# Attention with decay and a sticky mixture of experts on one core: heads 4 to 7 of the first batch turned by TensorE instead of DMA transposes

## The chip, the core and the metric

The kernel runs on one core of one Trainium2 chip. TensorE (PE) multiplies matrices, VectorE (DVE), ScalarE (ACT) and GpSimd (POOL) work on elements, and SyncE (SP) issues nearly all of the DMA transfers, from one queue. The metric is the time of one execution in device microseconds, the median of several runs.

## The reference, cut to what matters

```
scores = (q @ k^T) / sqrt(64) + cum[i] - cum[j]       # cum: running sum of log f; causal; 8 batches, 8 heads, 576 x 64
attn   = exp(scores - max) / sum;   x = attn @ v      # heads joined: 8 x 576 tokens of 512
logits = x @ w_gate;  expert of a token: argmax of its logits, or the expert of the token before it if its local gate says so
out    = p[e] * (relu(x @ w1[e]) @ w2[e])             # 8 experts, 512 -> 1024 -> 512
```

## The kernel before, in words

Every product is made from f16 halves (a high and a low part). For the scores TensorE needs q and k with the head dimension on the partitions, and they arrive with tokens on the partitions, so each head has to be turned twice: once with high and low part together (128 rows, into `Aq` and `Ak`), and once as the high part alone (64 rows) with the decay rows below it (rows 64 to 69, into `QB` and `KB`). One unit of attention (`cunit`, `aunit`, `bunit`, `d1unit`) multiplies `Ak,Aq`, then `KB,QB`, adds a mask (these are its scores, lines 935 and 942), takes the maximum on VectorE (`nm`, L946), the exponential on ScalarE (`P`, L966), is turned on TensorE (`pt`, L981), split into `ph` (ScalarE, L986) and `pl` (VectorE, L990), and multiplied with V (`xp`, L960). Batch 0 has 20 units of heads 0 to 7 in order, five for each pair of heads, then four `d1unit`s and one `d2unit` for the last 64 tokens. Two pools of PSUM banks feed them: `psS` (four banks: scores, and the 64-row turns of heads) and `psT` (two banks: `pt`, and the 128-row turns).

In batch 0, `heads` turns heads 0 and 1 before the first unit and `due_head` turns heads 2 and 3 between units: four 64-row turns (`turn_high`), a product that writes the decay rows (`add_decay`), four 128-row turns (`turn_first`), a copy by VectorE to `Aq` or `Ak` and one by ScalarE to `QB` or `KB` (`untwist`). Heads 4 to 7 go another way: GpSimd splits them (`pieces`), `turn` turns them by DMA transposes on SP's queue, `copy_hi` copies the high part from `Aq` and `Ak` to `QB` and `KB` by DMA, and `aug_main` fills in the decay rows from a copy in DRAM. In batch 1 and later, `prep_turned` turns groups of eight blocks on TensorE and a DMA copies the high part in two halves (heads 0 to 3, heads 4 to 7) and a last piece.

The order on each engine is made when the program is built. `issue` takes, time after time, the stage of a unit that could start first by a model of engine clocks; the list `DUE` names steps (`k2`: `due_head(2, "k")`; `v`, `v4`: a split of V by ScalarE and VectorE; `a`, `b`: the lists `ORDA` and `ORDB`) with a model time, at which a step is put ahead of whatever stage comes next. `ORD0`, `ORDA` and `ORDB` are written by hand: `q:p` splits the last tokens of q, `q0:m` loads half of batch 1's q, `q:t4` and `q:c` are the DMA transposes and copies of heads 4 to 7, `0:R` and `1:R` copy constant rows, `q0:P` is a half of batch 1's split, `q:2` loads for batch 2. Engines then run their lists strictly in that order.

Of the kernel before, what the change touches and what calls it, by code (L numbers as in the profile page):

```python
# [10 lines left out]
F16 = mybir.dt.float16  # L11
I32 = mybir.dt.int32
AF = mybir.ActivationFunctionType
ALU = mybir.AluOpType
# [25 lines left out]
def moves_of(d):  # L40
    return [tuple(x.split(":")) for x in d.split()]

ORD0 = moves_of("q:l :k2 :sv k:l q:t4 k:t4 :sp q:p q0:m k:p q:c k:c q1:m q:t q:M k:t :lm k:m :at 0:R 1:R :lv")
ORDA = moves_of("k:M q0:P 0:V 1:V k:ag")
ORDB = moves_of("q:ag q:G0 2:V q1:P k0:P k1:P k:e q:e 3:V q:G1 k:G0 :vl :Vl k:G1 q:2 :iv v0:P k:2")

GM, GW = 8, 500

# [23 lines left out]
SB = 3  # L74

T0 = 9700.0
DUE = (("k2", 11000), ("q2", 12500), ("k3", 14500), ("q3", 15000), ("v", 18000), ("v4", 19500), ("a", 26000), ("b", 30000))

TUNE = {
# [23 lines left out]
def kernel(  # L103
# [12 lines left out]
    nc = tc.nc  # L116
# [117 lines left out]
                load_main(0, nm, C, h0, h1)  # L234


    for c in range(2):
        nc.gpsimd.memset(QB[0][64:70, 16 * c + 8:16 * c + 16], -1.0)

    lg = cp.tile([64, S], F32, name="lg")  # L240
    cu = cp.tile([64, S], F32, name="cu")
    spm = cp.tile([64, 3, 512], F16, name="spm")
    spt = cp.tile([64, 3, 64], F16, name="spt")
    one = cp.tile([1, 1], F32, name="one")
    nc.vector.memset(one, 0.0)
    nc.vector.memset(KB[0][64:70, 16:32], 1.0)

    spk = cp.tile([97, 512], F16, name="spk")
    nc.gpsimd.memset(spk, 0.0)
    nc.gpsimd.memset(spk[96:97], 1.0)  # L250
    pick = cst.tile([97, 2, 4, 6], F16, name="pick")
    nc.gpsimd.memset(pick, 0.0)
    for t in (pick[:, 0, :, 3:6], pick[:, 1, :, 0:3]):
        nc.gpsimd.affine_select(out=t, in_=t, pattern=[[-1, 4], [-32, 3]], compare_op=ALU.not_equal, fill=1.0, base=0,
                                channel_multiplier=1)
    nc.gpsimd.memset(pick[96:97, 0, :, 0:3], -1.0)
    nc.gpsimd.memset(pick[96:97, 1, :, 3:6], 1.0)
# [14 lines left out]
    def decays():  # L272

        x = lg[:, 0:512]
        nc.vector.tensor_copy(spm[:, 1], x)
        nc.vector.tensor_tensor(x, x, spm[:, 1], ALU.subtract)
        nc.vector.tensor_copy(spk[64:68], x[0:4])
        nc.vector.tensor_copy(spm[:, 2], x)

    def last_parts():  # L280
# [102 lines left out]
    def aug_main(b, nm, h0, eng=nc.sync):  # L383
        B, src = Tq[b][nm + "B"], augm[:, b * H + h0:(b + 1) * H]
        if nm == "k":
            eng.dma_start(out=flat(B[64:67, 4 * h0:32]), in_=src.rearrange("j h x -> j (h x)"))
        for c in range(2 if nm == "q" else 0):
            eng.dma_start(out=flat(B[67:70, 16 * c + 2 * h0:16 * c + 16]).rearrange("p (g x) -> p g x", x=64),
                          in_=src.rearrange("j h (a c x) -> j c (h a) x", a=4, c=2)[:, c])
# [207 lines left out]
    def turn_high(h, nm):  # L597
        st, c0 = psS.tile([128, 512], F32, name="st"), 64 * (nm == "k")
        for a in range(4):
            nc.tensor.matmul(st[0:64, 128 * a:128 * a + 128], lhsT=Tq[0][nm + "t"][:, 4 * h + a, c0:c0 + 64], rhs=ident16,  # L600
                             start=(a == 0), stop=True, skip_group_check=True)
        return st
# [21 lines left out]
    def start():  # L624
        for nm in "qk":
            new_prep(0, nm)
        high("q", 0, 2, True)
        high("k", 0, 2)
        high("k", 2, 4)
        high("q", 2, 4)  # L630
        other_masks()
        for h in range(2):
            low("q", h, h + 1, nc.gpsimd, True)
            low("k", h, h + 1, nc.gpsimd)
        low("k", 2, 4, nc.gpsimd)
        load_v(0, groups=((0, 2),), last=False)
        by_chunks()
        decays()
        for j in range(2):
            nc.scalar.copy(spk[32 * j:32 * j + 4], spm[0:4, j])  # L640
        for C in range(2):
            load_main(0, "q", C, 4, 8)
        put_aug()
        heads(0)
        low("q", 2, 4, nc.vector)
        heads(1)
        split_v(0, 2, True)
        for C in range(2):
            load_main(0, "k", C, 4, 8)
        load_v(0, groups=((2, 8),), last=False)  # L650
        for nm in "kq":
            aug_main(0, nm, 4)

        for nm in "qk":
            for x in pieces(nm, 4, 8):
                x()
        for nm in "qk":
            LT[1, nm] = LT[0, nm]
            new_prep(1, nm)
        for x in ORD0:  # L660
            moves(x)

    def same_rows(i):

        t, a, n, g = ((QB, 64, 6, 8), (KB, 67, 3, 16))[i]
        y = 36 // n
        nc.sync.dma_start(out=flat(t[1][a:a + 3]).rearrange("p (n y) -> p n y", n=n),
                          in_=flat(t[0][a:a + 3, g:g + y]).unsqueeze(1).broadcast_to([3, n, 128 * y]))
# [105 lines left out]

    def due_head(h, nm):
        t = max([clock["PE"]] + [e + WAIT[src, "PE"] for r in ("psS", "psT") for e, src in [min(room[r])]])
        st = turn_high(h, nm)
        add_decay(st, h, nm)
        pt = turn_first(h, nm)
        untwist(nc.vector.tensor_copy, Tq[0][nm + "A"], pt, 128, h, nm)  # L780
        untwist(nc.scalar.copy, {"q": QB, "k": KB}[nm][0], st, 70, h, nm)
        clock["PE"] = t + 870
        for r, eng, c in ("psS", "ACT", 480), ("psT", "DVE", 330):
            room[r].remove(min(room[r]))
            clock[eng] = max(clock[eng], t + 1000) + c
            room[r].append((clock[eng], eng))
# [114 lines left out]
    def compute(b, T):  # L901
# [273 lines left out]
        if b < B - 1:  # L1175
            then(max(lb, lc, key=UO.index), lambda: finish_main(b, X["xn"]))
        else:
            F = []

            def some():  # L1180
                F.extend(finish_main(b, X["xn"]))
                F[0]()
                F[1]()

            then(lb, some)
            then(lc, lambda: F[2]())
        for i, u in enumerate(units if b > 1 else ()):
            u["needs"] = [(b, x, min(i // 10 * 2 + 1, 4) if i < 20 else 4) for x in "qk"]
        return [units[i] for i in UO]
# [24 lines left out]
    def start_of(st):  # L1214

        n, u, prev = line[st][0]
        eng, _, _, takes, _ = u[st]
        t = clock[eng]
        after = []
        if st == "tq":  # L1220
            after.append((u["ready"], "POOL"))
        elif st == "z0":
            if "w0" not in EX or "xt0" not in EX:
                return None
            after += [(EX["w0"], "POOL"), (EX["xt0"], "POOL")]
        elif prev is not None or st not in ("sc", "z0"):
            dep = (n, prev) if prev is not None else (n - 1, "ex")
            if dep not in ends:
                return None
            after.append(ends[dep])  # L1230
        if st == "sc":
            for key in u.get("needs", ()):
                if key not in turned:
                    return None
                after.append((turned[key] + 3500, "POOL"))
        for r, c in takes.items():
            if len(room[r]) < c:
                return None
            after += sorted(room[r])[:c]
        return max([t] + [e + WAIT.get((src, eng), 200) for e, src in after])  # L1240
# [56 lines left out]
    def issue(*until):  # L1297
        while any(line.values()):
            ready = [(start_of(st), line[st][0][0] + RANK[st], st) for st in STAGES if line[st]]
            if chain:  # L1300
                ready.append((side_next()[0], serial[0] + RANK["side"], "side"))
                W["side"] = side_weight(*side_next())
            t, _, st = min((x for x in ready if x[0] is not None), key=lambda x: (x[0] + W[x[2]], x[1]))
            if due and due[0][0] <= t and all(room[r] for r in due[0][2]):
                due.popleft()[1]()
                continue
            let_go(t)
            if st == "side":
                side_issue(*side_next())
                continue  # L1310
            n, u, prev = line[st].popleft()
            eng, cost, fn, takes, frees = u[st]
            for r, c in takes.items():
                for _ in range(c):
                    room[r].remove(min(room[r]))
            now[0] = t
            fn()
            clock[eng] = t + cost
            ends[n, st] = t + cost, eng
            if st == "eq":  # L1320
                turned[u["key"]] = t + cost
            for r, c in frees.items():
                room[r] += [ends[n, st]] * c
            if (n, st) == until:
                return

    turned = {}
    now = [0.0]

    def ends_at(eng, cost):  # L1330
# [482 lines left out]
    def open_small():  # L1813
# [5 lines left out]
    DO = {"k2": lambda: due_head(2, "k"), "q2": lambda: due_head(2, "q"), "k3": lambda: due_head(3, "k"),  # L1819
          "q3": lambda: due_head(3, "q"), "v": lambda: due_v(2, 4), "v4": lambda: due_v(4, 6), "v6": lambda: due_v(6, 8),  # L1820
          "a": due_a, "b": due_b, "nop": nop}
    due.extend((T, DO[f], ("psS", "psT") if f in ("k2", "k3", "q2", "q3") else ()) for f, T in DUE)

    NE = CAP + EARLY

# [798 lines left out]
```

## Time and profile before

| | |
|---|---|
| median of 3 runs | 803.95 us (803.55 to 807.25) |
| the profiled execution | 800.73 us, span 798.9 us |
| busy share of the span: PE, DVE, ACT, POOL | 94%, 63%, 55%, 51% |
| granted TensorE clock, mean over the span | 0.997 |

The span is the profiled stretch of the core; the execution's time has 1.8 us around it. The exponentials of attention end at about half of the span; the experts fill the rest. The change touches the first 80 us.

### The profile page before, as it was taken

The page shows a single profiled execution, that of the slowest core. Times are in us where ns is not written, and L with a number is a line of the kernel's source. Part 1 is how long each engine was busy: PE and PEld are TensorE (multiplying, and loading weights), DVE is VectorE, ACT ScalarE, POOL GpSimd, SP SyncE. Part 2 cuts the span into 40 slices and gives each one's busy share as a digit, 9 for nine tenths or more (in the row PEclk, how much of TensorE's full clock was granted, in tenths as well). Part 3 has the DMA queues.
Part 4 walks back from the last instruction along what each step waited for, and adds up shares of the span by engine and source line. Part 5 has one row for each costly group of instructions (what it writes and reads, how often), then busy time and mean ns, then how long its engine had stood idle before and what let it go on. Part 6 is the DMA issues. An engine that isn't in the chain of part 4 may idle for free. (4 is left out here: it accounts for less than half of the span.)

```text
span 798.9 us, 22025 instructions
## 1 busy us (share of the span) xinstructions
PE 752.1 (94%) x8972; PEld 542.0 (68%) x8972; DVE 503.0 (63%) x1142; ACT 435.6 (55%) x813; POOL 404.8 (51%) x471
## 2 busy tenths in 40 slices
PE   5799989999998989997899999999999999999996
PEld 3587878778787878875684565675665757666453
DVE  7688879799989899889969753352350524325010
ACT  5698968887786878776634224342341423324120
POOL 9698979295894869659617214121402213030101
PEclk9999999999999999999999999999999999999999
DMA  7967999686876868286495383775392744827101
GB/s 179 189 143 166 193 194 208 134 171 157 140 180 125 168 141 158 52 188 168 94 196 221 87 270 97 185 200 176 108 224 76 207 169 145 219 76 212 42 2 51
DMA packets 195338, 122.01 MB, mean 153 GB/s; under 512 B 135099, under 2 KB 171197, under 8 KB 195212
## 3 DMA queue, kind: packets, MB, share of 16 engines
q1 hardware_dynamic: 189169, 101.42, 56.0%
q0 software_dynamic: 6064, 19.14, 7.2%
q8 instruction: 72, 1.18, 0.6%
q14 instruction: 33, 0.27, 0.1%
HBM read 72.15 MB, written 19.36 MB: 115 GB/s over the span
## 5 line engine op out<-in xcount | busy, mean ns | idle before, releaser
L966 ACT ACTIVATE P<-st,nm 128x512 f32<-128x512 f32 (+3 forms) x288 | 152.8, 585 | 25.7 <-DVE nm L946 20.5
L1762 PE MATMUL z<-xT,wh 128*128 128x300 f16 (+7 forms) x832 | 144.6, 289 | 1.5 <-DVE hl L1749 1.5
L946 DVE TENSOR_REDUCE nm<-st 128x1 f32<-128x512 f32 (+4 forms) x264 | 134.1, 543 | 10.3 <-PE st L942 5.6
L986 ACT CAST ph<-pt 128x512 f16<-128x512 f32 (+1 forms) x200 | 115.7, 583 | 45.5 <-PE pt L981 41.2
L981 PE MATMUL pt<-ident,P 128*128 128x128 f32 x784 | 122.6, 279 | 8.2 <-DVE pl L990 5.4
L990 DVE TENSOR_TENSOR pl<-pt,ph 128x512 f16<-128x512 f32 (+1 forms) x171 | 114.3, 671 | 16.8 <-ACT ph L986 11.3
L1754 POOL DMA_INDIRECT out_dram<-o,ranki x23 | 23.9, 1039 | 160.3 <-ACT o L1753 139.0
L1749 DVE SCALAR_TENSOR_TENSOR hl<-z,hh 128x240 f16<-128x240 f32 (+7 forms) x64 | 42.2, 661 | 97.4 <-ACT hh L1748 97.4
L1789 PE MATMUL y<-uh,hh 128*128 128x512 f16 (+2 forms) x440 | 101.1, 311 | 0.0
L981 PEld LDWEIGHTS pt<-ident,P 128*128 128x128 f32 x784 | 84.3, 141 | 24.7 <-DVE pl L990 6.7
L1789 PE MATMUL y<-ul,hh 128*128 128x512 f16 (+2 forms) x440 | 100.8, 309 | 0.0
L1789 PE MATMUL y<-uh,hl 128*128 128x512 f16 (+2 forms) x440 | 100.8, 309 | 0.0
L1762 PEld LDWEIGHTS <-wh 128*128 128x128 f16 x832 | 81.0, 97 | 27.8 <-issue 2.1
L1762 PE MATMUL z<-xT,wl 128*128 128x300 f16 (+7 forms) x416 | 94.5, 289 | 0.0
L1789 PEld LDWEIGHTS <-hh 128*128 128x128 f16 (+2 forms) x880 | 56.8, 100 | 53.2 <-issue 5.2
L960 PE MATMUL xp<-VH,ph 128*128 128x65 f16 (+1 forms) x960 | 92.7, 196 | 0.0
L960 PE MATMUL xp<-VH,pl 128*128 128x65 f16 (+1 forms) x960 | 90.5, 194 | 1.8 <-DVE pl L990 1.7
L960 PE MATMUL xp<-VL,ph 128*128 128x65 f16 (+1 forms) x960 | 91.5, 195 | 0.0
L960 PEld LDWEIGHTS <-ph 128*128 128x128 f16 (+1 forms) x1920 | 83.3, 102 | 8.9 <-issue 4.9
L1748 ACT ACTIVATE hh<-z 128x240 f16<-128x240 f32 (+7 forms) x64 | 36.7, 574 | 93.5 <-PE z L1762 93.5
L935 PE MATMUL st<-KB,QB 70*128 70x256 f16 (+4 forms) x448 | 76.4, 278 | 5.1 <-DMA KB<-Ak 5.1
L935 PE MATMUL st<-Ak,Aq 128*128 128x256 f16 (+4 forms) x448 | 76.9, 281 | 2.4 <-ACT P L966 2.3
(369 smaller groups left out, 1404.9 us busy)
## 6 DMA issues: line engine op xcount, KB each, us to landing
stg<-in_moe_w_dram SPq DMA_DIRECT2D x64, 512.0 KB
xs<-xr SPq DMA_DIRECT2D x16, 512.0 KB
ldq<-in_q_dram SPq DMA_DIRECT2D x14, 512.0 KB
ldk<-in_k_dram SPq DMA_DIRECT2D x14, 512.0 KB
ldv<-in_v_dram SPq DMA_DIRECT2D x28, 256.0 KB
QB<-Aq SPq DMA_DIRECT2D x15, 256.0 KB
KB<-Ak SPq DMA_DIRECT2D x15, 256.0 KB
ldv<-in_v_dram SPq DMA_DIRECT2D x20, 64.0 KB
```

The lines of the kernel that those rows point to most:

```text
L935: nc.tensor.matmul(st[p0:p0 + m, co:co + n], lhsT=queries(lq, kk, h, c), rhs=rhs, start=(ps == 0 and first and co == col), stop=(ps == 1), ...
L946: nc.vector.tensor_reduce(dst, src, axis=AX.X, op=ALU.max, negate=True)
L960: nc.tensor.matmul(xo, lhsT=a[:, c0:c0 + m], rhs=w[:, vi, :], start=False, stop=(i == n - 1 and jj == 2), skip_group_check=True)
L966: nc.scalar.activation(P[:, c0:c1].rearrange("p (k x r) -> p k r x", r=2, x=64), st[:, c0:c1].rearrange("p (k r x) -> p k r x", r=2, x=64) ...
L981: nc.tensor.matmul(U["pt"][:, i * 128:(i + 1) * 128], lhsT=P[:, i * 128:(i + 1) * 128], rhs=ident, is_transpose=True, start=(i == 0), stop ...
L986: nc.scalar.copy(U["ph"][:, :cols], U["pt"][:, :cols])
L990: nc.vector.tensor_tensor(U["pl"][:, :cols], U["pt"][:, :cols], U["ph"][:, :cols], ALU.subtract)
L1748: nc.scalar.activation(hv, z[:, 0:nh, 0:wd], AF.Relu)
L1749: nc.vector.scalar_tensor_tensor(lv, z[:, 0:nh, 0:wd], 0.0, hv, ALU.max, ALU.subtract)
L1754: nc.gpsimd.indirect_dma_start(out=outf, out_offset=bass.IndirectOffsetOnAxis(ap=scat(t), axis=0), in_=o, in_offset=None, bounds_check=NT ...
L1762: nc.tensor.matmul(z[:, a, 0:wd], lhsT=w[:, d, fc * 128:(fc + 1) * 128], rhs=xT[:, x, a * wd:(a + 1) * wd], start=(i == 0), stop=(i == len ...
L1789: nc.tensor.matmul(y[m * r:m * r + m, 0:w], lhsT=a[:, fc, c0:c0 + m], rhs=u[:, fc, w * r:w * r + w], start=(i == 0), stop=(i == len(prods) ...
```

## The change

Heads 4 to 7 go through `due_head` too: eight more steps (`q4` to `q7`, `k4` to `k7`) stand in `DUE`, with model times around those of `k2` to `q3`, and the two splits of V come earlier in model time. The tile `pick`, which selects a head's decay rows, has eight heads in place of four. The DMA transposes, the DMA copies, the loads of decay rows and the constant rows (two memsets of 16 blocks in `QB` and `KB`) for heads 4 to 7 are gone. `same_rows` copies its constant rows from blocks of head 0 on, and the moves of batch 1 stand in another order. A unit of batch 0 is issued only when its heads have been.

```
-ORD0 = moves_of("q:l :k2 :sv k:l q:t4 k:t4 :sp q:p q0:m k:p q:c k:c q1:m q:t q:M k:t :lm k:m :at 0:R 1:R :lv")
-ORDA = moves_of("k:M q0:P 0:V 1:V k:ag")
-ORDB = moves_of("q:ag q:G0 2:V q1:P k0:P k1:P k:e q:e 3:V q:G1 k:G0 :vl :Vl k:G1 q:2 :iv v0:P k:2")
+ORD0 = moves_of(":k2 :sv q:l k:l :sp q:p q0:m k:p q1:m k:t q:t :lm q:M k:m :at :lv")
+ORDA = moves_of("k:M 0:V k:ag q0:P 1:V")
+ORDB = moves_of("0:R 1:R q:ag q:G0 q1:P 2:V k0:P k1:P k:e q:e 3:V q:G1 k:G0 :vl :Vl k:G1 q:2 :iv v0:P k:2")
...
-DUE = (("k2", 11000), ("q2", 12500), ("k3", 14500), ("q3", 15000), ("v", 18000), ("v4", 19500), ("a", 26000), ("b", 30000))
+DUE = (('k2', 11000), ('q2', 12500), ('k3', 14500), ('q3', 15000), ('q5', 15000), ('q4', 16000), ('k6', 16000), ('v', 16000), ('v4', 16500), ('k4', 17000), ('k5', 17000), ('q6', 20000), ('k7', 22000), ('q7', 23000), ('a', 26000), ('b', 30000))
...
-    for c in range(2):
-        nc.gpsimd.memset(QB[0][64:70, 16 * c + 8:16 * c + 16], -1.0)
...
-    nc.vector.memset(KB[0][64:70, 16:32], 1.0)
...
-        nc.vector.tensor_copy(spk[64:68], x[0:4])
+        nc.vector.tensor_copy(spk[64:72], x[0:8])
...
-        for nm in "kq":
-            aug_main(0, nm, 4)
...
-        t, a, n, g = ((QB, 64, 6, 8), (KB, 67, 3, 16))[i]
+        t, a, n, g = ((QB, 64, 6, 0), (KB, 67, 3, 0))[i]
...
+        headed.add((nm, h))
...
+            if any(x not in headed for x in u.get("heads", ())):
+                return None
...
+    for h in range(4, H):
+        for nm in "qk":
+            DO[f"{nm}{h}"] = lambda h=h, nm=nm: due_head(h, nm)
```

ScalarE's list shows how this comes out. Before, from the copy of q of head 2 on (`st` are turned heads and scores, `KB`, `QB` the targets of head copies, `P` the exponentials of units, `VH` the splits of V):

```order
L611 CAST QB_120<-st 70x4x2x64
L966 ACTIVATE P<-st,nm 128x4x2x64
L609 CAST KB_122<-st 70x512
L611 CAST QB_120<-st 70x4x2x64
L966 ACTIVATE P<-st,nm 128x2x64
L966 ACTIVATE P<-st,nm 128x3x2x64
L986 CAST ph<-pt 128x512
L318 CAST VH_124<-ldv 128x4x2x64
```

ScalarE's list of the changed kernel from the same place, the copy of q of head 2:

```order
L607 CAST QB_120<-st 70x4x2x64
L960 ACTIVATE P<-st,nm 128x4x2x64
L605 CAST KB_122<-st 70x512
L607 CAST QB_120<-st 70x4x2x64 x3
L605 CAST KB_122<-st 70x512
L314 CAST VH_124<-ldv 128x4x2x64 x2
L605 CAST KB_122<-st 70x512 x2
L607 CAST QB_120<-st 70x4x2x64
L605 CAST KB_122<-st 70x512
L607 CAST QB_120<-st 70x4x2x64
L960 ACTIVATE P<-st,nm 128x2x64
```

The eight new head copies and both splits of V stand together, right after head 3, ahead of the second unit's exponential. TensorE's list has the eight heads at the same place; before, after the last turn of head 3's q, it went on with the fourth unit's scores:

```order
L594 LDWEIGHTS t16q
L594 MATMUL pt<-ident_72,t16q 128x128
L935 LDWEIGHTS Aq
L935 MATMUL st<-Ak,Aq 128x256
L935 LDWEIGHTS Aq
```

In the changed kernel TensorE goes on, after the last turn of the last head (q of head 7), with those same scores:

```order
L590 LDWEIGHTS t16q
L590 MATMUL pt<-ident_72,t16q 128x128
L929 LDWEIGHTS Aq
L929 MATMUL st<-Ak,Aq 128x256
L929 LDWEIGHTS QB_120
```

So all eight heads are turned before the fourth unit's scores. Around the change of batches SP's list moves too. Before, it issued batch 1's copies of the high part of k (`KB_123<-Ak`: heads 0 to 3, heads 4 to 7, the last piece), then batch 2's loads (`ldq`, `ldk`, `ldv`):

```order
L422 DMA KB_123<-Ak 64x2048 x2
L429 DMA KB_123<-Ak 64x512
L192 DMA ldq<-in_q_dram 128x8x128 x2
L199 DMA ldq<-in_q_dram 64x4x64 x2
L192 DMA ldk<-in_k_dram 128x8x128 x2
L199 DMA ldk<-in_k_dram 64x4x64 x2
L212 DMA ldv<-in_v_dram 128x8x64 x4
```

SP's list of the changed kernel, with the same copies and loads:

```order
L418 DMA KB_123<-Ak 64x2048
L192 DMA ldq<-in_q_dram 128x8x128 x2
L199 DMA ldq<-in_q_dram 64x4x64 x2
L192 DMA ldk<-in_k_dram 128x8x128 x2
L199 DMA ldk<-in_k_dram 64x4x64 x2
L212 DMA ldv<-in_v_dram 128x8x64 x2
L418 DMA KB_123<-Ak 64x2048
L212 DMA ldv<-in_v_dram 128x8x64
L425 DMA KB_123<-Ak 64x512
```

The copy for heads 4 to 7 and the last piece now stand behind ten and eleven of batch 2's loads.

## Rows read from the trace of the kernel before

**Rows 1.** The page: the span, and busy time of the engines.

```profile
span 798.9 us, 22025 instructions
...
PE 752.1 (94%) x8972; PEld 542.0 (68%) x8972; DVE 503.0 (63%) x1142; ACT 435.6 (55%) x813; POOL 404.8 (51%) x471
```

**Rows 2.** Who waited for whom, 0 to 60 us: total, times, longest (us).

```profile
PE st L935 <- DMA KB<-Ak: 3.8, 1, 3.8
...
PE xp L960 <- DVE pl L990: 1.7, 1, 1.7
...
DVE ft L258 <- DMA ft<-in_f_dram: 0.7, 1, 0.7
```

**Rows 3.** Stretches: us; PE, PEld, DVE, ACT, POOL busy; PEclk, DMA share, GB/s.

```profile
35.00:40.00 5.00, 4.62 (x51) 4.23 (x50) 1.68 (x5) 2.13 (x5) 2.56 (x3) 0.66 1.33 222
...
65.00:70.00 5.00, 4.07 (x80) 3.06 (x77) 3.94 (x10) 4.13 (x9) 4.75 (x6) 1.00 0.34 72
70.00:75.00 5.00, 5.00 (x91) 4.11 (x88) 4.76 (x11) 4.05 (x10) 2.49 (x3) 1.00 1.14 280
...
80.00:100.00 20.00, 19.88 (x317) 16.40 (x315) 16.05 (x38) 18.26 (x37) 19.38 (x21) 1.00 0.93 194
100.00:120.00 20.00, 17.37 (x334) 14.72 (x333) 14.41 (x32) 13.67 (x30) 14.80 (x40) 1.00 0.95 194
```

**Rows 4.** Timeline of TensorE, 0 to 60 us: start, duration (us), instruction, count.

```profile
12.10 0.64 PE L600 MATMUL st<-ident,t16k 128*64 128x128 f16 x4
...
14.05 1.01 PE L605 MATMUL st<-spk,pick 97*6 97x512 f16 x2
15.00 0.51 PE L935 MATMUL st<-Ak,Aq 128*128 128x512 f16 x1
...
20.75 0.41 PE L600 MATMUL st<-ident,t16q 128*64 128x128 f16 x4
21.09 0.38 PE L605 MATMUL st<-spk,pick 97*6 97x512 f16 x1
...
21.63 0.38 PE L935 MATMUL st<-Ak,Aq 128*128 128x256 f16 x2
...
35.38 0.38 PE L935 MATMUL st<-KB,QB 70*128 70x512 f16 x1 [3.84 <-DMA KB<-Ak]
```

**Rows 5.** Timeline of ScalarE: a head copy, a V split, a turned group, `ph`.

```profile
21.50 0.58 ACT L611 CAST QB<-st 70x512 f16<-70x512 f32 x1 [0.61 <-PE st L605]
...
23.31 0.63 ACT L318 CAST VH<-ldv 128x512 f16<-128x512 f32 x1
...
64.56 1.03 ACT L514 ACTIVATE Ak<-st 128x1024 f16<-128x1024 f16 x1
...
68.57 0.59 ACT L986 CAST ph<-pt 128x512 f16<-128x512 f32 x1 [0.41 <-PE pt L981]
```

**Rows 6.** Timeline of VectorE: a head copy, two V splits, `pl`.

```profile
21.30 0.41 DVE L609 COPY Ak<-pt 128x512 f16<-128x512 f16 x1
...
23.97 1.57 DVE L319 TENSOR_TENSOR VL<-ldv,VH 128x512 f16<-128x512 f32 x1 [0.89 <-ACT VH L318]
...
26.66 0.68 DVE L319 TENSOR_TENSOR VL<-ldv,VH 128x512 f16<-128x512 f32 x1
...
66.50 0.68 DVE L990 TENSOR_TENSOR pl<-pt,ph 128x512 f16<-128x512 f32 x1
```

**Rows 7.** Timeline of SP's queue: issue start and duration (us), transfer, count.

```profile
29.55 0.51 SPq L422 DMA_DIRECT2D KB<-Ak  x1
...
68.05 1.23 SPq L192 DMA_DIRECT2D ldq<-in_q_dram  x2
...
76.80 4.84 SPq L212 DMA_DIRECT2D ldv<-in_v_dram  x4
```

**Rows 8.** Timeline of TensorE in batch 1: scores of its first unit and of head 4's first.

```profile
69.22 0.38 PE L935 MATMUL st<-Ak,Aq 128*128 128x512 f16 x1
...
78.11 0.39 PE L935 MATMUL st<-Ak,Aq 128*128 128x512 f16 x1
```

More of the change, by code (lines that the diff above doesn't have):

```diff
@@ L250 @@
     nc.gpsimd.memset(spk[96:97], 1.0)
-    pick = cst.tile([97, 2, 4, 6], F16, name="pick")
+    pick = cst.tile([97, 2, 8, 6], F16, name="pick")
     nc.gpsimd.memset(pick, 0.0)
     for t in (pick[:, 0, :, 3:6], pick[:, 1, :, 0:3]):
-        nc.gpsimd.affine_select(out=t, in_=t, pattern=[[-1, 4], [-32, 3]], compare_op=ALU.not_equal, fill=1.0, base=0,
+        nc.gpsimd.affine_select(out=t, in_=t, pattern=[[-1, 8], [-32, 3]], compare_op=ALU.not_equal, fill=1.0, base=0,
                                 channel_multiplier=1)
@@ L639, in start @@
         for j in range(2):
-            nc.scalar.copy(spk[32 * j:32 * j + 4], spm[0:4, j])
+            nc.scalar.copy(spk[32 * j:32 * j + 8], spm[0:8, j])
         for C in range(2):
@@ L1186, in compute @@
             then(lc, lambda: F[2]())
+        for i, u in enumerate(units[0:20] if b == 0 else ()):
+            h = i // 5 * 2 + (i % 5 > 1)
+            u["heads"] = [(x, y) for x in "qk" for y in ((h, h - 1) if i % 5 == 3 else (h,))]
         for i, u in enumerate(units if b > 1 else ()):
@@ L1302, in issue @@
                 W["side"] = side_weight(*side_next())
-            t, _, st = min((x for x in ready if x[0] is not None), key=lambda x: (x[0] + W[x[2]], x[1]))
+            able = [x for x in ready if x[0] is not None]
+            if not able:
+                due.popleft()[1]()
+                continue
+            t, _, st = min(able, key=lambda x: (x[0] + W[x[2]], x[1]))
             if due and due[0][0] <= t and all(room[r] for r in due[0][2]):
@@ L1327 @@
     turned = {}
+    headed = {(x, h) for x in "qk" for h in range(2)}
     now = [0.0]
@@ L1821 @@
           "a": due_a, "b": due_b, "nop": nop}
-    due.extend((T, DO[f], ("psS", "psT") if f in ("k2", "k3", "q2", "q3") else ()) for f, T in DUE)
+    for h in range(4, H):
+        for nm in "qk":
+            DO[f"{nm}{h}"] = lambda h=h, nm=nm: due_head(h, nm)
+    due.extend((T, DO[f], ("psS", "psT") if f[0] in "qk" else ()) for f, T in DUE)
     NE = CAP + EARLY
```

## The prediction

> **What bounds the kernel now.** I read the page first: TensorE is busy for 94% of the span, no other engine for more than 63% [rows 1]. So a saving counts where TensorE stands idle or runs slowly, and every microsecond of work added to TensorE is paid unless it falls into a gap. Then the list of waits for the first 60 us [rows 2]: two waits there touch the change. TensorE waits 3.8 us for the DMA copy `KB<-Ak`, the high part of k of heads 4 to 7; and it waits 1.7 us for a `pl`, whose engine, VectorE, has a split of V ahead of it (23.97, 1.57 us [rows 6]). Third, the table of stretches [rows 3]: from 35 to 40 us, behind that stall, the granted clock is 0.66 on the mean, while it is 1.00 around it: TensorE had stood idle, and part of this stretch ran at 1.2 GHz instead of 2.4. From 80 to 100 us TensorE is busy for 19.88 of 20 us and ScalarE for 18.26: in a steady batch nothing is left over in which lost time could be made up.
>
> **What goes.** The stall of 3.84 us ending at 35.38 [rows 4] goes, since `KB` of heads 4 to 7 no longer comes by DMA: -3.8. The slow clock behind it goes with it: 0.34 of 5 us of full-speed work were not done [rows 3], -1.7; if the clock fell for another reason it stays, so 0 to -1.7. The wait of 1.7 us for `pl` goes, because both splits of V now stand among the heads and no longer ahead of the first `pl`: -1.7, or 0 if the first units are held up by something else. The two memsets gone at the start give nothing: VectorE's first real operation waits for a DMA anyway (`ft`, 0.7 us [rows 2]), and everything up to TensorE's first head hangs on that; were this cover not there, VectorE's memset would count. The shorter DMA work of the first 30 us lets batch 1's loads start earlier; nobody in the rows waits for them.
>
> **What comes.** Eight heads' tensors on TensorE. One of them, q of head 3, takes from 20.75 to 21.63, 0.88 us, with nothing in the way [rows 4]; eight take 7.0 us. They stand in one block, ahead of the fourth unit's scores, where TensorE has no gap to hide them. ScalarE's copies are 0.58 us each and its two splits of V 0.63 [rows 5], together 5.9 us; VectorE's copies are 0.41 [rows 6], 3.3 us, and its two splits 1.4 to 3.1. Both fit beside 7.0 us, but the splits stand in the middle, behind the copy for k of head 6, and what is queued behind them are the copies of k of head 4. TensorE can go two tensors further, since two `psS` banks and two `psT` banks are free for heads (two `psS` banks hold scores). Counting forward with these durations, the third tensor behind the splits waits some 0.4 us for ScalarE, and then for VectorE 0.3 us where a split takes 0.68 and 1.9 us where it takes 1.57. The short one is the row at the time in question (26.66 [rows 6]), so I take 0.7 us in all: +7.7, bounds 7.0 and 9.3.
>
> Together the first batch gives 7.7 - 3.8 - 1.7 - 1.7 = +0.5 us. Bounds: 7.0 - 7.2 = -0.2, and 9.3 - 5.5 = +3.8 with the wait for `pl` not won back.
>
> On the clock in this block: heads 0 and 1 ran at the lower level (two `pick` products took 1.01 us at 14.05, where one took 0.38 at 21.09), and with just this mix of turns ahead of it the clock was at the higher level from the first scores on; head 3 was turned at it [rows 4]. The Trainium skill's page "TensorE: Matmul & The Clock Gate", Part 4 (PE-mode transpose), says on the other hand that the full clock does not engage for transposes; by it the run of heads would be turned at the slow rate, which is the third rival below. The trace does not bear it out for heads 0 to 3, whose nine matmuls hold four real transposes.
>
> **What moves.** SP's list around the change of batches is what I take most from. Batch 1's second copy of the high part of k (heads 4 to 7) stood ahead of batch 2's loads; now ten of them stand between it and the first copy. Call x the time at which SP issues the first of these loads, right behind the first copy, which it may issue once ScalarE has copied k's second group. From x SP needs, at the pace that it had for the same ten loads, 76.80 - 68.05 + 4.84/2 = 11.2 us [rows 7]. Then the second copy is issued. The one such copy that was waited for took from 29.55 [rows 7] to 35.38 [rows 4], 5.8 us, with loads in front of it in the queue. So it is usable at about x + 17.0. At the other end, by bytes alone: 4 x 512 + 4 x 64 + 2 x 256 KB of loads and 256 KB of the copy are 3.15 MB, which at 280 GB/s [rows 3] are 11.2 us.
>
> When does TensorE want it? Behind k's second group ScalarE has one more group (1.03), two `ph` (0.59 each [rows 5]) and VectorE one `pl` (0.68 [rows 6]) until the last full unit of batch 0 can be multiplied with V; with 0.6 us for those products batch 1's first scores come 3.5 us after the second group's copy, which is x + 2.9 (the first copy's issue takes 0.5 [rows 7]). Head 4's first scores came 78.11 - 69.22 = 8.9 us after batch 1's first [rows 8], so at x + 11.8. TensorE would then stand for 17.0 - 11.8 = 5.2 us by the one end and not at all by the other. SP's pace shows that the queue, not the bytes at their best rate, sets the time, so I go near the upper end, and somewhat below it because the copy of 29.55 had DMA transposes in the queue before it, which are gone: +4.0, bounds 0 and 5.2. What is queued behind that matmul is all of TensorE's list, so ScalarE and VectorE run dry as they did at 35 us. The stall is as long as the one that is removed, so I expect the same slow clock behind it: +1.7, bounds 0 and 1.7.
>
> The other moves I cost at nothing: the last tokens of q and k, the DMA transposes of those, the constant rows and the gate weights are issued earlier or at about their old time, and their users come some 20 us later; without that cover the price would be a DMA's issue to use, the 5.8 us above. GpSimd has two memsets less and starts batch 1's split earlier, for which nobody waited.
>
> **Sum.** +0.5 + 4.0 + 1.7 = +6.2 us. The profiled execution took 800.7 us (span 798.9), so 806.9 for one like it. The median of the runs shown is 803.95, 3.2 above the profiled one; the same difference laid on it gives 810.2, and I say 810. Differences below 0.5% (4.0 us) can hardly be told from none: the runs shown spread over 3.7 us.
>
> **Rivals.**
>
> 1. *The second copy of k lands in time*, since SP issues faster with fewer transfers in flight, or batch 1's start is later than I think against x. For it: the bound by bytes is x + 11.2, before the need at x + 11.8. Against it: SP's measured pace. Then the first batch's +0.5 is all: 804.5.
>
> 2. *Not slower: batch 1 flows better.* TensorE has gaps of 0.93 us between 65 and 70 us and of 2.63 us between 100 and 120 [rows 3], around the changes of batches. If GpSimd's and the loads' lead of some microseconds closes both, and the second copy is in time, the result is -0.2 - 0.9 - 2.6 = -3.7: 800.2. Point at which it decides: the copy is issued by x + 6.0 (11.8 - 5.8), so that nothing stalls. Against it: none of those gaps waits for GpSimd in the list of waits.
>
> 3. *The block of heads is slower than eight times 0.88.* By the clock at its lower level, two tensors took 15.00 - 12.10 = 2.90 us [rows 4], 1.45 each, 0.57 more than at the higher: 8 x 0.57 = 4.6, so 0.5 + 4.6 = +5.1 with no second stall: 809; with it above 814. The slow splits of V alone would bring +1.6 or, with the wait not won back, +3.3.
>
> **How the numbers follow.** The forecast, with a stall of at least 2 us in batch 1: 0.52. Rival 1: 0.27. Rival 2: 0.13. Rival 3: 0.08. The forecast's own range is 806.0 (a stall of 2 us, no slow clock behind it: +2.5 and half a microsecond of the first batch less) to 813.5 (+3.8 + 4.0 + 1.7); rivals 1 and 2 lie below. The range for 8 in 10 must reach rival 1 and part of rival 2 and leave out the worst sums: 802 to 813.5. Slower by over 0.5% is most of the forecast and rival 3: 0.47 + 0.08 = 0.55. Within 0.5%: the forecast's lower edge, rival 1 and some of rival 2: 0.05 + 0.25 + 0.03 = 0.33. Faster by over 0.5%: what is left of rival 2 and a little of rival 1 in which ScalarE rather than TensorE sets the pace: 0.12.
>
> **What the profile after would show.** The wait of TensorE for `KB<-Ak` at 31 us gone, and the granted clock at 1.00 from 15 us to the end of batch 0. A block of eight tensors of about 0.95 us each from 21.6 to 29.3 us, in it waits for ScalarE and VectorE of under 1 us. The fourth unit's scores at about 29.3, and batch 1's first scores near 70, 0 to 2 us later than before. Then the step that decides: some 9 us later a wait of TensorE for `KB<-Ak` of 2 to 5 us, SP issuing that copy some 11 us behind the first load of batch 2, and a clock below 1.00 behind it. I am wrong if that wait is not there (then rival 1 or 2), if the block of heads takes 12 us or its matmuls show the slow pace (rival 3), or if batch 1's first scores come before 68 us, for then TensorE had room that the busy rows do not show.

## The result, and the profile after

The changed kernel takes 809.98 us (median of 10 executions, 807.04 to 816.77) against 805.46 us (10 executions, 801.07 to 807.25): a ratio of 1.0068, 95% interval 1.0047 to 1.0089. It is slower: by 4.5 us between the medians, by 5.5 us by the ratio. Its profiled execution took 807.84 us with a span of 806.1, 7.2 above that of before. The lines of the kernel have moved: scores L935 is now L929, the turns L600/L594 are L596/L590, the copies of k on SyncE's queue L422/L429 are L418/L425.

The waits of TensorE in the changed kernel, first from 0 to 60 us, then from 66 to 150 us (total, times, longest):

```profile
PE st L596 <- ACT t16k L571: 8.2, 1, 8.2
PE st L601 <- ACT spk L636: 0.6, 1, 0.6
...
PE st L929 <- DMA KB<-Ak: 5.7, 1, 5.7
PE pt L975 <- DVE pl L984: 0.7, 2, 0.4
PE xp L944 <- DVE xn L1019: 0.3, 1, 0.3
```

Both waits of [rows 2] that the change was about, 3.8 us for `KB<-Ak` and 1.7 us for `pl`, are gone from the first list. The second is led by a wait for the same transfer one batch later, 5.75 us. It shows in TensorE's timeline (start, duration, instruction): the last turn of head 3 and the first of the eight new ones, the fourth unit's scores, and in batch 1 the first scores, head 4's first and the matmul that waited.

```profile
20.76 0.41 PE L596 MATMUL st<-ident,t16q 128*64 128x128 f16 x4
...
21.74 0.41 PE L596 MATMUL st<-ident,t16q 128*64 128x128 f16 x4
...
29.65 0.38 PE L929 MATMUL st<-Ak,Aq 128*128 128x256 f16 x2
...
68.39 0.38 PE L929 MATMUL st<-Ak,Aq 128*128 128x512 f16 x1
...
77.44 0.39 PE L929 MATMUL st<-Ak,Aq 128*128 128x512 f16 x1
...
83.58 0.58 PE L929 MATMUL st<-KB,QB 70*128 70x512 f16 x1 [5.75 <-DMA KB<-Ak]
```

Eight turns take 21.74 to 29.65, 7.91 us, 0.98 each with a single gap of 0.2. The fourth unit's scores came at 21.63 before [rows 4], so 8.02 us are spent; yet batch 1's first scores stand at 68.39 instead of 69.22 [rows 8]. The first batch gained 0.83 us. Everything is lost behind that, on SyncE's queue (issue start and duration, transfer, count):

```profile
65.63 0.48 SPq L418 DMA_DIRECT2D KB<-Ak  x1
66.16 1.52 SPq L192 DMA_DIRECT2D ldq<-in_q_dram  x2
67.74 3.05 SPq L199 DMA_DIRECT2D ldq<-in_q_dram  x2
70.83 2.15 SPq L192 DMA_DIRECT2D ldk<-in_k_dram  x2
73.02 2.30 SPq L199 DMA_DIRECT2D ldk<-in_k_dram  x2
75.43 1.95 SPq L212 DMA_DIRECT2D ldv<-in_v_dram  x2
77.47 1.84 SPq L418 DMA_DIRECT2D KB<-Ak  x1
```

The second copy of k's high part is issued at 77.47, behind ten loads of batch 2; TensorE had come to it at 77.83. The table of stretches (us; PE, PEld, DVE, ACT, POOL busy; PEclk, DMA share, GB/s) shows the rest:

```profile
35.00:40.00 5.00, 5.00 (x75) 4.37 (x76) 4.91 (x11) 4.70 (x12) 4.02 (x3) 1.00 0.98 244
80.00:85.00 5.00, 1.43 (x6) 0.86 (x5) 0.00 (x0) 0.00 (x0) 4.92 (x5) 0.59 1.01 182
85.00:90.00 5.00, 5.00 (x57) 4.33 (x57) 2.70 (x6) 3.04 (x6) 4.92 (x5) 0.73 0.76 140
100.00:120.00 20.00, 19.32 (x358) 16.33 (x358) 15.30 (x36) 17.79 (x37) 8.38 (x34) 1.00 0.68 140
```

From 35 to 40 us the clock is 1.00 (0.66 before [rows 3]); instead it falls while TensorE stands at 81 us, and TensorE works at 1.2 GHz until 87.7, some 4.2 us, of which 2.1 are lost. From 80 to 85 us VectorE and ScalarE do nothing: everything hangs on the one copy. From 100 to 120 us TensorE is busy for 19.32 us, 1.95 more than before.

**One instruction as a milestone.** ScalarE's turned group of k near 250 us is the same instruction in both kernels. These are its rows before and after, and in two runs told below (both copies first; old kernel with the late copy):

```profile
250.02 1.01 ACT L514 ACTIVATE Ak<-st 128x1024 f16<-128x1024 f16 x1
...
254.71 1.01 ACT L510 ACTIVATE Ak<-st 128x1024 f16<-128x1024 f16 x1
...
250.17 1.01 ACT L510 ACTIVATE Ak<-st 128x1024 f16<-128x1024 f16 x1
...
257.37 1.01 ACT L514 ACTIVATE Ak<-st 128x1024 f16<-128x1024 f16 x1
```

The changed kernel is 4.69 us late here: -0.83 + 5.75 + 2.1 = +7.0, and then -1.95 by two waits of the kernel before that it doesn't have:

```profile
109.22 0.42 PE L883 MATMUL st<-wg,xlt 128*64 128x18 f16 x8 [0.73 <-DMA xlt<-xl]
...
116.17 0.38 PE L935 MATMUL st<-KB,QB 70*128 70x512 f16 x1 [1.22 <-DMA KB<-Ak]
```

That makes 5.1; 0.4 I can't assign. Counted from batch 1's first scores, which takes out what differed earlier, the way to this row is 180.80 us before, 186.32 in the changed kernel, 182.77 and 187.43 in the two runs. By its end the profiled execution is 7.2 late; the 2.5 us beyond the milestone hold a stretch at the lower clock at 367 to 371 us, which before doesn't show, and two gaps of 0.43 us near 560 and 610 us that wait for nothing in the profile. No row ties them to the change.

### The profile page after: what moved, and what is told of

It reads as the page before. It is cut to its first block, busy times and chain, and to the rows that moved or that the text cites. A ratio compares the mean times of both kernels' runs of the same rounds, so it can differ in the third digit from the quotient of the medians.

```text
span 806.1 us, 22172 instructions
## 1 busy us (share of the span) xinstructions
PE 761.5 (94%) x9044; PEld 548.0 (68%) x9044; DVE 499.4 (62%) x1149; ACT 439.9 (55%) x821; POOL 403.8 (50%) x469
## 5 line engine op out<-in xcount | busy, mean ns | idle before, releaser
L929 PE MATMUL st<-KB,QB 70*128 70x256 f16 (+4 forms) x448 | 77.3, 280 | 5.7 <-DMA KB<-Ak 5.7
L929 PE MATMUL st<-Ak,Aq 128*128 128x256 f16 (+4 forms) x448 | 77.7, 283 | 2.0 <-ACT P L960 1.8
```

The costliest lines, as they stand in the source:

```text
L929: nc.tensor.matmul(st[p0:p0 + m, co:co + n], lhsT=queries(lq, kk, h, c), rhs=rhs, start=(ps == 0 and first and co == col), stop=(ps == 1), ...
```

## The experiments

The theory: the slower time is the late copy on SyncE's queue, not the turning of four heads on TensorE. The rival: the turns cost what the queue's wait seems to cost. Each run is compared with the kernel before on the same chip; the traces are of one execution each; "start" is batch 1's first scores (69.22 before, 68.39 after), "milestone" the row near 250 us.

**Both copies first.** The changed kernel, and where batch 1 begins:

```diff
         if b == 1:
+            let_go(1e12)
             while bulk and bulk[0][0] == 0:
                 bulk.popleft()[2]()
```

> The changed kernel (809.98 us) with one call added where batch 1 begins: both copies of k for heads 4 to 7 of batch 1 are issued on SyncE's queue ahead of batch 2's loads. Theory A (the late copy is what costs): the 5.75 us wait for KB<-Ak at the sixth unit of batch 1 is gone, and with it the half clock behind it (about 2 us): 7 to 8 us less than the changed kernel, 802 to 804.5 us, so level with the kernel before (805.46) or up to 0.5% faster. Theory B (the turning of heads 4 to 7 on TensorE costs what was gained, and the queue is only a shift): the wait closes but the time stays within 2 us of 810. Theory C (half of it): the loads of batch 2 are now later by the copies' issue (1 to 2 us) and the wait moves to batch 2: 805 to 808 us, with a new wait near the start of batch 2.

Measured: 806.68 us, ratio 1.0025 (0.9995 to 1.0056). The copies' wait is gone from TensorE's list, and so is the half clock at 81 us. Start 67.40, milestone 250.17: 4.54 us ahead of the changed kernel, level with the kernel before. But 0.99 of this was there before the added call acts: the fourth unit's scores stand at 28.66 in this execution and at 29.65 in that of the changed kernel. From start to milestone the call returns 3.55 us, half of theory A's 7 to 8. The time lies in theory C's range, and as in theory C a new wait stands near the change to batch 2, though for another transfer than its loads. TensorE's timeline of this run shows it:

```profile
108.86 0.51 PE L877 MATMUL st<-wg,xlt 128*64 128x18 f16 x8 [1.94 <-DMA xlt<-xl]
```

and behind it the clock falls (stretches of the same run, columns as above):

```profile
108.00:109.00 1.00, 0.14 (x4) 0.14 (x5) 0.00 (x0) 0.23 (x1) 1.00 (x2) 1.00 0.88 218
109.00:113.00 4.00, 4.00 (x52) 3.91 (x51) 0.30 (x3) 1.34 (x4) 0.60 (x1) 0.57 0.90 195
```

1.94 us of waiting and 0.43 of 4 us (1.7 us) of slow clock are new; the changed kernel had neither. Yet SyncE's queue issued the transpose `xlt<-xl` at about the same time before, in the changed kernel and in this run:

```profile
105.05 1.92 SPq L848 DMA_TRANSPOSE xlt<-xl  x1
104.64 1.30 SPq L842 DMA_TRANSPOSE xlt<-xl  x1
104.38 1.29 SPq L842 DMA_TRANSPOSE xlt<-xl  x1
```

In the changed kernel the queue had gone on while TensorE stood at 81 us, and so this transfer was in time there.

**The old kernel with the late copy.** The kernel before; on the queue the copy for heads 4 to 7 stands behind ten of batch 2's loads, as in the changed kernel (the last piece stays ahead of them):

```diff
-                    hold_back(ends_at(eng, cost), lambda: copy_hi(b, nm, 2 * j - 2, 2 * j + 2))
+                    hold_back(1e9 if (b, nm, j) == (1, "k", 3) else ends_at(eng, cost), lambda: copy_hi(b, nm, 2 * j - 2, 2 * j + 2))
...
+            if b == 1 and i == 2:
+                let_go(1e9)
```

> The kernel before (805.46 us) with only the queue's order of the changed kernel: the second copy of k for heads 4 to 7 of batch 1 is issued behind ten of batch 2's loads, heads 4 to 7 of batch 0 still by DMA. Theory A (that order alone makes the kernel slower): a wait for KB<-Ak of 5 to 6 us at the sixth unit of batch 1, and about 2 us of half clock behind it: 5.5 to 8 us more than before, 811 to 813.5 us. Theory B (the wait comes of the batch that runs earlier in the changed kernel, not of the queue): under 2 us more than before.

Measured: 811.83 us, ratio 1.0088 (1.0059 to 1.0118), theory A. TensorE's row in batch 1:

```profile
85.58 0.58 PE L935 MATMUL st<-KB,QB 70*128 70x512 f16 x1 [6.36 <-DMA KB<-Ak]
```

Start 69.94, milestone 257.37, 7.35 us late. Of this 0.72 stands at start already, ahead of the edit (the wait in the first batch was 4.60 us in this execution instead of 3.84); 6.63 come behind it. With heads 4 to 7 of batch 0 left to the DMA, the queue's order alone makes the kernel slower. And here too the two waits of before at 109 and 116 us are gone:

```profile
100.00:120.00 20.00, 20.00 (x338) 16.92 (x336) 15.10 (x34) 17.98 (x38) 8.37 (x34) 1.00 0.73 144
```

**The load behind.** The kernel before; half of batch 1's q (a load of 512 KB) stands behind the copies for heads 4 to 7 of batch 0:

```diff
-ORD0 = moves_of("... :sp q:p q0:m k:p q:c k:c q1:m q:t ...")
+ORD0 = moves_of("... :sp q:p k:p q:c k:c q0:m q1:m q:t ...")
```

> The kernel before (805.46 us) with one move changed: batch 1's q load of 512 KB, which stands ahead of the copies for heads 4 to 7 of batch 0 on SyncE's queue, stands behind them. Theory A (the 3.84 us wait for KB<-Ak in the first batch is the queue's): the wait shrinks by some 2 us (512 KB at about 245 GB/s), and the half clock behind it (1.7 us) shrinks or goes: 2 to 4 us less than before, 801.5 to 803.5 us. Theory B (the wait is for the transposes ahead of the copies): within 0.7 us of before.

Measured: 801.89 us, ratio 0.9974 (0.994 to 1.0008). The wait shrinks from 3.84 us [rows 4] to

```profile
32.60 0.38 PE L935 MATMUL st<-KB,QB 70*128 70x512 f16 x1 [1.58 <-DMA KB<-Ak]
```

and the clock stays at 1.00 from 35 to 40 us. The copy itself is issued no earlier than before (29.55 [rows 7]):

```profile
29.51 0.51 SPq L422 DMA_DIRECT2D KB<-Ak  x1
```

It is usable 3.1 us after its issue, against 5.8 before, with the load in front of it. Start 65.85, 3.37 us ahead; milestone 247.36, 2.66 ahead, with a new wait of 0.85 us at 55.29 for decay rows (`QB<-augt`) between. Theory A: 2.26 us of the wait and the slow clock behind it go with one move of one load, where the change spent 8 us of TensorE's time. The time agrees, but its interval reaches 1.

**Two heads.** As the run with both copies first, but heads 6 and 7 by DMA as before:

```diff
-ORD0 = moves_of(":k2 :sv q:l k:l :sp q:p q0:m k:p q1:m k:t q:t ...")
+ORD0 = moves_of(":k2 :sv q:l k:l q0:m q1:m q:t4 k:t4 :sp q:p k:p q:c k:c k:t q:t ...")
```

> As the run with both copies first, but only heads 4 and 5 of batch 0 are turned on TensorE; heads 6 and 7 go by DMA transposes and copies as in the kernel before, and land ahead of need by the queue's rows (needed about 44 us after the start). Theory A (TensorE sets the pace in the block of head units, 0.98 us a unit): four units less, 3.9 us less than the run with both copies first, 798 to 801 us. Theory B (ScalarE sets it, 0.48 us a unit): 1.9 us less. Theory C (the copies for heads 6 and 7 land late): a wait for KB<-Ak in the first batch of 2 to 4 us and its half clock, so level with or slower than the run with both copies first.

Measured: 803.88 us, ratio 0.9981 (0.9951 to 1.0012); against the run with both copies first 2.8 us less by the medians. Start 64.42 against 67.40: 2.98 us less. That lies between theory A's 3.9 and theory B's 1.9, and the time misses theory A's 798 to 801. Four turns at 0.98 are 3.92; of these 0.86 comes back as a wait right behind the block, where TensorE turns the first unit's exponentials,

```profile
25.65 0.65 PE L981 MATMUL pt<-ident,P 128*128 128x128 f32 x4 [0.86 <-DVE Ak L609]
```

which leaves 3.06. By the rows TensorE sets the pace inside the block (theory A's mechanism), and the copies for heads 6 and 7 are in time (no wait for `KB` in the first batch).

**V behind the heads.** As the run with both copies first, V's two splits due at 24.0 and 24.5 us instead of 16.0 and 16.5.

> As the run with both copies first, but the splits of V (due 16.0 and 16.5 us) are due after the last unit of heads (24.0 and 24.5 us), so that they stand behind the heads again. Theory A (their earlier place is what removed the wait for pl at the first pt of the first batch, counted 1.7 us): a wait of 1 to 1.7 us for pl or for VH is back between 22 and 32 us, and batch 1 starts 1.0 to 1.7 us later than in the run with both copies first. Theory B (the block of heads gives them time wherever they stand): no such wait, batch 1 starts within 0.4 us of it.

One execution, profiled: 810.29 us. Start 70.19, 2.8 us later than in the run with both copies first, more than theory A's 1.7. TensorE waits again, but for ScalarE's `P` and not for `pl`:

```profile
32.49 0.38 PE L929 MATMUL st<-Ak,Aq 128*128 128x512 f16 x1 [1.63 <-ACT P L960]
```

A piece of 0.5 us was there already when this run's heads began (17.60 for a turn that stands at 17.06 there), which leaves 2.3. The planner also put the fourth unit's scores ahead of the last two heads' turns here, so not all of it is V's. The 4.2 us that it waits for `xlt` in batch 1 add to its time. That the earlier place of V's splits pays is likely; how much is not shown by this one execution.

**V earlier in the old kernel.** The run with the load behind, V's splits due at 16.0 and 16.5 us.

> The kernel before with batch 1's q load behind the copies, and the splits of V due at 16.0 and 16.5 us; the transposes stay where they were. Theory A (a stall that goes shows again at the next late thing): the wait for pl of 1.18 us goes and the wait for KB<-Ak grows from 1.58 to 2.5 to 2.8 us, batch 1 starts within 0.4 us of the run with the load behind alone. Theory B: the wait for KB<-Ak stays below 2 us and batch 1 starts 0.8 us or more earlier.

One execution: 816.25 us. The wait for `pl` is gone and that for `KB` in the first batch is 2.66 us, as theory A has it, but start is 68.41, 2.56 us later. Behind 2.66 us the clock fell, where behind 1.58 it had not:

```profile
30.00:40.00 10.00, 7.34 (x73) 6.35 (x73) 4.12 (x9) 3.35 (x8) 4.56 (x7) 0.66 1.02 236
```

From the matmul that waited (32.74) the lower level lasts until 38.8 us, 6.0 us of work of which 3.0 are lost; that alone is more than the delay of start. Then SyncE's queue reads

```profile
67.23 0.48 SPq L422 DMA_DIRECT2D KB<-Ak  x1
67.77 1.53 SPq L192 DMA_DIRECT2D ldq<-in_q_dram  x2
...
76.59 3.67 SPq L212 DMA_DIRECT2D ldv<-in_v_dram  x3
80.36 1.02 SPq L422 DMA_DIRECT2D KB<-Ak  x1
```

and TensorE waits 5.74 us for that second copy. Neither theory had the slow clock or the second wait. No head was turned on TensorE here: two due times alone put the copy behind eleven loads. So the late copy isn't tied to the heads; the planner's clock in the program decides whether the copy is let go before the loads are sent, and in the kernel before it is.

**Transposes earlier, and with V.** The run with the load behind, and `q:t4 k:t4` ahead of `q:l k:l` (these two now behind `:k2 :sv`, as in the changed kernel); the second run has V's splits at 16.0 and 16.5 as well.

> The kernel before with batch 1's q load behind the copies, as in the run of that name, and with the DMA transposes for heads 4 to 7 of batch 0 issued ahead of the last chunks' loads of q and k instead of behind them. The q transposes can then be issued at 17.7 us (their input's end on GpSimd) instead of 19.96. Theory A: the 1.58 us that was left of the wait for KB<-Ak goes, batch 1 starts 1.3 to 1.6 us earlier than there, 800 to 801.5 us and so 0.5 to 0.7% under the kernel before. Theory B (GpSimd's pieces of the last chunk now wait for their late load, and the pieces and masks behind them): the wait goes but another of 1 us or more stands later in batch 0; 801 to 803 us.

> As the run with the transposes earlier, and the splits of V due at 16.0 and 16.5 us (before: 18.0 and 19.5). Theory A: the wait of 1.2 us for pl at 25.7 us goes too; with the copies 2.2 us earlier they still land about in time: batch 1 starts 0.8 to 1.2 us earlier than in that run, 799 to 800.5 us, 0.6 to 0.8% under the kernel before. Theory B (the stall only moves: TensorE reaches the copies 1.2 us sooner and waits for them as much longer): no change against that run.

Transposes earlier: 801.99 us, ratio 0.9962 (0.9941 to 0.9982), the only interval that lies below 1. But start is 65.91 and the wait for `KB` 1.81 us, much as with the load behind alone (65.85, 1.58): theory A's 1.3 us did not come. The copy of k is issued at 28.20 instead of 29.51, and is usable at 32.59 instead of 32.60. Whether this version is better than the load behind alone stays open. With V earlier: 811.98 us, ratio 1.0113 (1.008 to 1.0146); start 69.70, and a wait of 6.0 us for `KB` in batch 1, as in the run before. The late start has other reasons, also of that kind: waits of 2.2 us for `KB` (with the lower clock behind it, 0.83 from 30 to 40 us) and 2.5 us for `QB<-augt` in the first batch. Both theories fall.

**Held transfers first, everywhere.** Since the run with both copies first waited for `xlt<-xl`, which stands behind eight loads of batch 3, the rule was made general: whatever is held back goes ahead of every group of loads. Once on the run with both copies first, once on that with the load behind:

```diff
         while bulk and bulk[0][0] <= i and bulk[0][1]():
+            let_go(1e12)
             bulk.popleft()[2]()
```

> As the run with both copies first, and in every batch what is held back (copies of k, transposes of x) is issued ahead of the next group of loads, when a group is taken. Theory A (one queue is behind both waits: what the removed wait gave back in batch 1 was lost again because the transpose of xl stands behind eight of batch 3's loads): the wait for xlt of 1.94 us at 109 us and the half clock behind it go, and batch 2 begins 1.5 to 3.5 us earlier than in the run with both copies first; 803 to 805 us. Theory B (those loads are themselves needed in time: held to the side by the copies' waits they land later): the xlt wait goes and waits for ldq or KB of 2 us or more appear in batches 2 to 5; 806 to 810 us.

> The kernel before with batch 1's q load behind the copies, and with the same rule for what is held back as in the run just named. Theory A: its waits for xlt (1.16 us) and for KB in batch 2 (1.22 us) go, batch 3 begins 1.5 to 2.4 us earlier than in the run with the load behind alone; 799 to 801 us, 0.5 to 0.8% under the kernel before. Theory B as there: new waits of 2 us or more in batches 2 to 5; 802 us or more.

Measured: 832.08 us, ratio 1.0369 (1.0343 to 1.0395), and 823.15 us, 1.0259 (1.0228 to 1.0289): theory A falls in both, and B's 806 to 810 us is far too low for the first (the second meets B's 802 or more). The waits of SyncE's own queue in the first of the two, 75 to 125 us, show why:

```profile
SPq L422 <- DVE pl L985: 6.4, 1, 6.4
SPq L422 <- DVE Aq L513: 3.5, 1, 3.5
SPq L808 <- POOL t16q L354: 3.5, 1, 3.5
SPq L808 <- POOL t16q L358: 2.8, 1, 2.8
```

The queue stands still for transfers whose input isn't ready, and the loads stand behind them; the wait for `xlt` grew to 4.7 us. The planner's later choices changed too, so not all of the 25 us against the run with both copies first is laid to these waits.

**One move.** The clean form of that test: only batch 1's `xlt<-xl`, ready at 92.1 us, goes behind the first of batch 3's eight loads instead of behind all. The order on the other engines is the same row by row.

```diff
         while bulk and bulk[0][0] <= i and bulk[0][1]():
+            while ahead and any(x[2] is ahead[0][0] for x in held):
+                ahead.pop()[1]()
             bulk.popleft()[2]()
```

> As the run with both copies first, and a single move on SyncE's queue: batch 1's transpose xlt<-xl and the two stores of xl stand behind the first of batch 3's eight loads of q and k instead of behind all eight; no other engine's order differs by a row. Its input is ready at 92.1 us, so the queue does not stand still for it. Theory A (the queue's order is what the removed wait turned into): the 1.94 us wait for xlt at 109 us is gone, with it the half clock at 109 to 112 us (1.7 us): by 250 us it is 2 to 3.5 us ahead of the run with both copies first, 803 to 805 us. Theory B (batch 3's loads, now 2.8 us later, are the next to be late, or TensorE is held there by something else that is done at about the same time): under 1 us ahead by 250 us.

> The kernel before with batch 1's q load behind the copies, and the same single move of xlt<-xl. Theory A: its wait for xlt (1.16 us) is gone; the wait for KB in batch 2 (1.22 us) then grows by as much or stays, so 0 to 1.2 us ahead of the run with the load behind alone by 250 us: 800.5 to 802 us, 0.3 to 0.6% under the kernel before. Theory B: no change against that run, or later by 1 us or more.

On the run with both copies first: 804.04 us, ratio 1.0026 (1.0003 to 1.0048), the same as without the move. The wait for `xlt` is gone, and in its place stands

```profile
115.85 0.50 PE L940 MATMUL st<-KB,QB 70*128 70x512 f16 x1 [3.55 <-DMA KB<-Ak]
```

with the clock at its lower level behind it. Milestone 251.09, 0.92 us later than without the move: theory B. On the run with the load behind: 800.01 us, ratio 0.9977 (0.9953 to 1.0001); milestone 249.63 against 247.36, with two stretches of lower clock before it where that run had none. One of them, and 1.01 us of the delay, stand ahead of the edit: in this execution the first batch's wait for `KB` was 2.66 us instead of 1.58, and start 66.86. No gain is shown either way.

## Why the prediction was right, by its steps

The mechanism held: the removed waits are gone, and a stall for the late copy stands in batch 1. That 810 us was met to 0.02 is luck. The forecast was +6.2 us on a median of 803.95 (3 executions); measured are +4.5 on a median of 805.46 (10 executions). Three terms lie outside their own bounds, the first batch (-0.83, lower bound -0.2), the stall (5.75, upper bound 5.2) and the clock (2.1, upper bound 1.7), and a term of -1.95 was missing; these errors partly cancel.

- **What goes.** Right: wait of 3.84 us, slow clock of 1.7 and wait for `pl` of 1.7 are gone from the rows. That V's place was worth its term is not shown alone: put back, batch 1 starts 2.8 us later, 0.5 of it from before and with other stages moved.
- **The block of heads.** Counted 7.7 us; 7.91 measured. Rival 3 is refuted by the durations: four 64-row turns take 0.41 us throughout the block, as for head 3, where they took 0.64 at 12.10 [rows 4]. The granted clock of the stretch (1.00 from 20 to 30 us) can't decide it, since the rows of before give 1.00 from 10 to 15 us as well, where the matmuls ran at half pace. The Trainium skill's "TensorE: Matmul & The Clock Gate", Part 4 (PE-mode transpose), says that the full clock doesn't engage for transposes; in this block, in which four matmuls of nine are transposes, the full pace stayed for 12.6 us of turns (17.06 to 29.65). For heads 0 and 1 the prediction says more than its rows show: their turns, 8.97 to 15.0 us, all ran at half pace. But in the run with both copies first the pace rose on turns alone: two `pick` products at 13.43, ahead of any scores, take 0.59 us in place of 1.01.
- **First batch +0.5.** Too high: -0.83, and in two later executions with the same order up to there (both copies first, one move) batch 1 starts at 67.40 and 67.21, before the 68 us that the prediction named as a sign of being wrong. The first of them is 0.99 us ahead already at the fourth unit's scores; from there both it and the changed kernel take 38.74 us. In the kernel before this way took 47.59 us, so 8.85 went where I had counted 7.24. 0.64 of the difference are the gaps around 65 to 70 us (0.93 before [rows 3], 0.29 now), a part of rival 2; the other 1.0 I can't assign.
- **The late copy.** Issue at x + 11.3 (counted 11.2), usable at x + 17.4 (17.0), with x = 66.16. Head 4's first scores stand at x + 11.3 (11.8), and the matmul behind them, the one that needs the copy, would have run at x + 11.7. The step that failed is the choice "somewhat below" the upper end, on the ground that transposes no longer stood in front of the copy: it took 6.1 us from issue to use, not less than the 5.8 of before. So 5.75 instead of 4.0, and rival 1 is refuted. The 5.8 was itself not the copy's own: with the load behind it is 3.1.
- **The slow clock behind it.** 2.1 instead of 1.7.
- **Not in the sum.** A stall stops TensorE, not the queue: the transfers needed at 109 and 116 us were then in time, and 1.95 us of the kernel before's own waits vanished, in the old kernel with the late copy too. Rival 2 had priced this gap at 2.6 us, but for the case without a stall. The run with both copies first shows the reverse: where the 5.75 us go, 1.94 and 1.7 come back, and moved away from there they come back as 3.55.

That the queue's order is the cause is shown from both sides: put into the old kernel it costs 6.63 us from start to milestone (6.4 by the medians), taken out of the changed one it returns 3.55 (the ratio to the kernel before falls from 1.0068 to 1.0025). Of the rest of theory A's 7 to 8 us, 3.6 is the queue's next late transfer with the slow clock behind it. In the changed kernel without the late copy, the turned heads neither gain nor lose measurably (1.0025, 0.9995 to 1.0056).

## What to carry to other kernels

When a transfer is late, look first at what stands in front of it in its queue: moving one 512 KB load took 2.3 of 3.8 us of the stall, and the slow clock behind it, that the change paid for with 8 us of TensorE's time. On a full queue like this one a next late transfer came up behind each wait that was removed, so price a removed wait only up to there, by following one and the same instruction in both traces; and a transfer moved ahead must have its input ready, or all that is behind it waits (up to 6.4 us here). Where a planner's clock decides an order, compare the whole order after any change of its inputs: here two due times of another tensor moved the copy behind eleven loads.

## What the runs showed of the hardware

A stall can cost more than its wait: behind 3.84 us of standing still TensorE ran at 1.2 GHz until 39.2 us, behind 5.75 until 87.7, behind 1.94 at 109 us for 3.4 us, while behind 0.73 us at the same place in the kernel before, and behind 1.58 in the run with the load behind, the clock stayed at 1.00. The same wait need not cost the same: behind 2.66 us for `KB` in the first batch the clock is 0.66 from 30 to 40 us in one execution (V earlier in the old kernel) and 0.83 in another (one move, load behind). How many such stretches fall into an execution differs from one to the next for the same kernel: 32 executions of the kernel before have mean granted clocks from 0.980 to 0.997, with 810.9 us at the one end and 801.3 us at the other. The profiled one of before is at 0.997, which fits its place 4.7 us under the median beside it. A milestone in the trace shows where a difference of 3 us arises, as medians don't, but it is of one execution: look in the rows ahead of it for stretches of lower clock and for what differed before the edit acts.
